# Writing the folded tiles of an FFT-like mixing stage component-major instead of feature-major

## The chip, the cores and the metric

The kernel runs on one core of a Trainium2 chip. The time is device microseconds (us) of one execution of the whole program, and the figure given for a kernel is the median of its runs. Engines are called by the profile's short names: PE (TensorE matmul) with PEld (its weight load), DVE (VectorE), ACT (ScalarE), POOL (GpSimd) and SP (SyncE).

## The reference, cut to what matters

Two dense transforms of an input `x` of 8 x 3072 x 256, of which the real part goes into a feed-forward layer with a maximum over three projections:

```python
X = np.fft.fft(x, axis=1)          # x: (8, 3072, 256), over the 3072 positions
X = np.fft.fft(X, axis=2)          # over the 256 features
a = X.real.reshape(24576, 256)
h = np.maximum(np.maximum(a @ w1, a @ w2), a @ w3)   # w1, w2, w3: (256, 768)
out = h @ w_out                                      # w_out: (768, 256)
```

## The kernel before, in words

The work goes batch by batch, 8 batches of 3072 positions. A batch has a transform part (`fnet`) and a feed-forward part of three blocks of 512 columns (the loop over `blk`), each with 6 chunks `jc` of the 768 hidden features.

`fnet` splits the length-3072 transform as 24 x 128. Its steps, with the lines that the prediction uses:

- Stage 1 (L270): 64 matmuls per batch transform 24 points, with columns of `x0` as the stationary operand. Each result group goes through a PSUM tile of the pool `ps_f`, which has two buffers, and ACT casts it to bf16 into `ub` (L272), in 13 pieces per batch in the order of the table `DLS`.
- The fold (L280, and single columns at L289 to L297): DVE adds and subtracts mirrored feature columns of `ub` and writes the sums into `zE` and the differences into `zO`. In `ub` 24 components of one feature lie side by side. Per batch there are 4 instructions of 25 x 24 elements, 8 of 10 x 24 and 8 of 9 x 24, half of each into `zE`. They can start as the pieces of `ub` arrive: first features 20 to 44, then 10 to 19 and 45 to 54, then the rest.
- Stage 2 (L318, L321 on `zE`; L324, L326 on `zO`; L332 to L334 for the middle position): 128-point transforms. Each matmul takes one component r of all 128 folded features as its stationary operand, `er[:, :, r]` or `orr[:, :, r]`. They fill six PSUM tiles per batch from the same two buffers of `ps_f` (three for `zE`, three for `zO`, 8 or 10 matmuls each), and ACT casts each to bf16 `tE` or `tO` (L329). So the third tile can be filled only when ACT has cast the first, and so on.

One matmul of stage 2 needs every feature of `zE` (or `zO`), so the first L318 waits for the last instruction of the fold that writes `zE`, the copy at L292.

The feed-forward part of a block: L349 and L350 (and L357 for the mirrored half) into PSUM tiles `pse`, ACT's Relu into `stmp` (L363), DVE's maximum into `hp` or `hm` (L364), and then the output products L367, L369 and 6 times L372 into the PSUM tile `po` of a pool with two buffers, which DVE copies to `ot` (L392) and SP stores.

What sets the order: on each engine instructions run in the order in which the building framework's scheduler put them, which is fixed when the kernel is built. The output products of the earlier block stand in a queue (`l2_queue`), so the scheduler has matmuls at hand to put between those of `fnet`; they are called fillers below. A new `po` can be written only when DVE has copied the one before the last.

Of the kernel before, what the change touches and what calls it, by code (L numbers as in the profile page):

```python
# [34 lines left out]
def kernel(  # L35
# [16 lines left out]
    nc = tc.nc  # L52
# [44 lines left out]
    def load_x0(b, between):  # L97
        x0 = x0_pool.tile([96, 128 * 64], BF16, name="x0", tag="x0")
        xr = x[b].rearrange("(a bb) (g dl) -> g a bb dl", bb=128, g=4)
        x0v = x0.rearrange("p (bb dl) -> p bb dl", dl=64)  # L100
        for ch in range(4):
            if ch in between:
                between[ch]()
            for g in range(4):
                nc.gpsimd.dma_start(  # L105
                    out=x0v[g * 24:(g + 1) * 24, ch * 32:(ch + 1) * 32, :],
                    in_=xr[g, :, ch * 32:(ch + 1) * 32, :])
        return x0
# [15 lines left out]
    dvec = gen.tile([128, 128], FP32, tag="dvec")  # L124

    def between():

        nc.gpsimd.iota(kidx, [[1, 13], [24, 128]], base=0, channel_multiplier=0,
                       allow_small_or_imprecise_dtypes=True)
        nc.gpsimd.iota(dvec, [[1, 64], [64, 2]], base=0, channel_multiplier=0,  # L130
                       allow_small_or_imprecise_dtypes=True)

    with tc.manual_schedule(engines={mybir.EngineType.Pool}):
# [80 lines left out]
    zO_tiles = [consts.tile([128, 128 * 26], BF16, name=f"zO{i}", tag=f"zO{i}")  # L214
                for i in range(1)]
    for zO in zO_tiles:
        nc.vector.memset(zO.rearrange("p (c r) -> p c r", r=26)[:, :, 24:26], 0.0)
        nc.vector.memset(zO[:, 0:26], 0.0)

    def prep_first():  # L220

# [42 lines left out]
    def fnet(b, x0):  # L264
# [9 lines left out]
        u = ub.rearrange("p (dl g r) -> p dl g r", g=4, r=24)  # L274
        zE = z_pool.tile([128, 128 * 24], BF16, name="zE", tag="zE")
        zO = zO_tiles[b % len(zO_tiles)]
        e = zE.rearrange("p (dl g r) -> p dl g r", g=2, r=24)
        o = zO.rearrange("p (dl g r) -> p dl g r", g=2, r=26)
        def fold(dst, op, lo, hi, g):
            nc.vector.tensor_tensor(out=dst[:, lo:hi, g, 0:24], in0=u[:, lo:hi, g, :],  # L280
                                    in1=u[:, 64 - lo:64 - hi:-1, 3 - g, :], op=op)
# [14 lines left out]
        nc.vector.tensor_copy(o[:, 0, 0, 13:24], u[:, 0, 2, 1:12])  # L296
        nc.vector.tensor_copy(o[:, 0, 0, 24:26], u[:, 0, 2, 0:13:12])  # L297

        er = zE.rearrange("p (c r) -> p c r", r=24)
        orr = zO.rearrange("p (c r) -> p c r", r=26)  # L300

        def iO(r):
            return 24 if r == 0 else 25 if r == 12 else 12 + r
# [121 lines left out]

    for b in range(B):
        tt = fnet(b, x0_tiles.pop(b))
        if b == 0:
            prep_first()
# [60 lines left out]
```

## Time and profile before

| | |
|---|---|
| median of 3 runs | 500.29 us (499.56 to 500.31) |
| the profiled execution's own time | 499.23 us |
| its span, first to last instruction | 497.1 us |
| mean granted TensorE clock | 0.993 |
| busy: PE, PEld, DVE, ACT, POOL | 453.5, 315.6, 320.4, 260.9, 140.6 us |

Matmuls are pipelined: their records overlap, so how fast PE goes is read from the distance between starts and not from the length of a record. In a timeline the first number of a row is the start and the second how long the row's instructions took together, both in us; a bracket says how long the engine sat idle before and what released it.

### The profile page before, as it was taken

What the parts mean: (1) busy time and instruction counts of PE and PEld (TensorE: products, weight loads), DVE (VectorE), ACT (ScalarE), POOL (GpSimd) and SP (SyncE); (2) the same over time, 40 slices, a digit from 0 to 9 for tenths busy, and PEclk for the clock granted to TensorE, in tenths of its full rate; (3) what the DMA queues carried; (4) which work ended last, traced back from release to release, by engine and by line L of the source; (5) the groups of instructions that cost most, each with busy time, mean ns of one, the idle gap of its engine ahead of it and who ended that gap; (6) DMA issues with size and microseconds to landing.
All of it is one profiled execution on the core that took longest, in us unless ns stands there. A gap on an engine that the chain in (4) does not pass through costs nothing.

```text
span 497.1 us, 9195 instructions
## 1 busy us (share of the span) xinstructions
PE 453.5 (91%) x3408; PEld 315.6 (63%) x3408; DVE 320.4 (64%) x662; ACT 260.9 (52%) x472; POOL 140.6 (28%) x160
## 2 busy tenths in 40 slices
PE   0056999999999999999999999999999999999995
PEld 0055447785568657785669666875669566866664
DVE  8834674657676576657666567657675666667663
ACT  1355652575436653575446644665457644765440
POOL 9979800029000750029000840048000100020000
PEclk9999899999999999999999999999999999999998
DMA  8999992219921692219911793119911022102122
GB/s 48 75 164 99 98 32 86 84 44 108 105 86 66 59 133 99 73 44 109 126 65 65 74 123 102 65 46 120 134 64 65 22 65 84 65 22 65 65 84 86
DMA packets 163436, 40.05 MB, mean 81 GB/s; under 512 B 136512, under 2 KB 163392, under 8 KB 163392
## 3 DMA queue, kind: packets, MB, share of 16 engines
q0 software_dynamic: 135536, 14.30, 70.6%
q1 hardware_dynamic: 27856, 25.18, 16.1%
q8 instruction: 26, 0.43, 0.4%
q14 instruction: 18, 0.15, 0.1%
HBM read 28.31 MB, written 25.17 MB: 108 GB/s over the span
## 4 chain that ended last, share of the span: by engine, by line
PE 78%; DVE 3%; ACT 2%; POOL 2%; DMA 1%; issue 1%; DVEq 0%; ACTq 0%
PE po L372 23%; PE pse L349 12%; PE pse L357 11%; PE pse L350 11%; PE ps L270 8%; PE po L367 4%; PE po L369 4%; POOL x L105 2%; PE ps L318 2%; DMA x<-in_x_dram 1%; PE ps L324 1%; PE ps L326 1%; ACT stmp L363 1%; PE ps L321 1%; DVE zE L280 1%
## 5 line engine op out<-in xcount | busy, mean ns | idle before, releaser
L363 ACT ACTIVATE stmp<-pse 128x512 bf16<-128x512 f32 (+1 forms) x294 | 167.7, 588 | 164.3 <-PE pse L350 128.6
L364 DVE TENSOR_TENSOR hp<-pse,stmp 128x512 bf16<-128x512 f32 x144 | 99.1, 690 | 99.1 <-PE pse L357 39.8
L105 POOL DMA_DIRECT2D x<-in_x_dram x128 | 109.5, 863 | 8.1 <-DMA x<-in_x_dram 3.6
L349 PE MATMUL pse<-tE,gE 128*128 128x512 bf16 x288 | 108.8, 379 | 1.7 <-DVE hm L364 0.7
L350 PE MATMUL pse<-tO,gO 128*128 128x512 bf16 x288 | 109.1, 380 | 0.0
L364 DVE TENSOR_TENSOR hm<-pse,stmp 128x512 bf16<-128x512 f32 x144 | 99.0, 687 | 11.8 <-ACT stmp L363 9.3
L357 PE MATMUL pse<-tO,gD 128*128 128x512 bf16 x288 | 94.8, 380 | 1.1 <-ACT stmp L363 0.6
L339 POOL COPY tEr<-tE 128x1536 bf16<-128x1536 bf16 x8 | 11.8, 1471 | 289.1 <-ACT tE L329 289.1
L372 PE MATMUL po<-wout_bf,hp 128*128 128x256 bf16 x576 | 92.6, 272 | 0.0
L372 PE MATMUL po<-wout_bf,hm 128*128 128x256 bf16 x576 | 89.1, 272 | 0.1
L270 PE MATMUL ps<-m24blk,x 96*128 96x96 bf16 x512 | 57.4, 250 | 28.8 <-DMA w_bf<-in_moe_w_dram 27.5
L270 PEld LDWEIGHTS <-x 96*128 96x128 bf16 x512 | 55.9, 199 | 33.1 <-DMA w_bf<-in_moe_w_dram 27.4
L392 DVE COPY ot<-po 128x512 f32<-128x512 f32 x96 | 65.5, 684 | 14.5 <-PE po L372 13.8
L372 PEld LDWEIGHTS <-hm 128*128 128x128 bf16 x576 | 56.1, 99 | 17.3 <-DVE hm L364 0.4
L372 PEld LDWEIGHTS <-hp 128*128 128x128 bf16 x576 | 56.2, 100 | 14.2
L272 ACT CAST ub<-ps 128x480 bf16<-128x480 f32 (+1 forms) x104 | 55.4, 554 | 15.6 <-PE ps L270 13.3
L357 PEld LDWEIGHTS <-gD 128*128 128x128 bf16 x288 | 28.1, 98 | 29.8 <-issue 1.5
L350 PEld LDWEIGHTS <-gO 128*128 128x128 bf16 x300 | 29.4, 98 | 27.1 <-issue 12.2
L349 PEld LDWEIGHTS <-gE 128*128 128x128 bf16 x300 | 29.5, 99 | 21.1 <-issue 2.6
L280 DVE TENSOR_TENSOR zE<-ub 128x240 bf16<-128x240 bf16 (+2 forms) x80 | 20.2, 311 | 33.9 <-ACT ub L272 33.9
L367 PE MATMUL po<-gw,tE 128*128 128x256 bf16 x96 | 26.2, 272 | 0.0
L369 PE MATMUL po<-gwr,tOr 128*128 128x256 bf16 x96 | 26.2, 272 | 0.0
(99 smaller groups left out, 359.5 us busy)
## 6 DMA issues: line engine op xcount, KB each, us to landing
out_dram<-ot SPq DMA_DIRECT2D x176, 128.0 KB, 1.7
x<-in_x_dram POOLq DMA_DIRECT2D x128, 96.0 KB, 6.7
out_dram<-ot SPq DMA_DIRECT2D x24, 64.0 KB, 6.7
w_bf<-in_moe_w_dram POOLq DMA_DIRECT2D x6, 192.0 KB, 6.2
out_dram<-ot SPq DMA_DIRECT2D x8, 63.0 KB
wout_bf<-in_moe_w_out_dram POOLq DMA_DIRECT2D x1, 384.0 KB, 8.6
out_dram<-ot SPq DMA_DIRECT2D x1, 8.0 KB
```

The source lines that it names most:

```text
L105: nc.gpsimd.dma_start(out=x0v[g * 24:(g + 1) * 24, ch * 32:(ch + 1) * 32, :], in_=xr[g, :, ch * 32:(ch + 1) * 32, :])
L270: nc.tensor.matmul(ps1[:, i * 96:(i + 1) * 96], x0r[:, :, d0 + i], m24blk, start=True, stop=True)
L272: nc.scalar.copy(out=ub[:, d0 * 96:d1 * 96], in_=ps1[:, 0:(d1 - d0) * 96])
L349: nc.tensor.matmul(pse[:, 0:n], gE[i][:, js], te, start=True, stop=False)
L350: nc.tensor.matmul(pse[:, 0:n], gO[i][:, js], to, start=False, stop=True)
L357: nc.tensor.matmul(pse, gD[i][:, js], to, start=False, stop=True, skip_group_check=True)
L363: nc.scalar.activation(out=stmp[:, 0:n], in_=pses[0][:, 0:n], func=AX.Relu)
L364: nc.vector.tensor_tensor(out=dst, in0=src3, in1=stmp[:, 0:n], op=ALU.max)
L367: nc.tensor.matmul(po, te, gw[:, 0:256], start=True, stop=False)
L369: nc.tensor.matmul(po, to, wo, start=False, stop=False)
L372: nc.tensor.matmul(po, hcols(jc), wout_bf[:, jc * 256:(jc + 1) * 256], start=False, stop=(jc == NJC - 1))
L392: nc.vector.tensor_copy(out=ot, in_=po)
```

## The change

`zE` and `zO` keep their sizes, but the order of their elements changes. Before, element (feature c = 2 dl + g, component r) stood at c x 24 + r (26 for `zO`); now the component is the outer index and the feature c = 64 g + dl the inner one. The table `dvec` that builds the second transform's matrix follows the new numbering of features, and the two zeroing memsets follow the new places.

```diff
-        nc.gpsimd.iota(dvec, [[1, 64], [64, 2]], base=0, channel_multiplier=0,
+        nc.gpsimd.iota(dvec, [[1, 128]], base=0, channel_multiplier=0,
...
-        nc.vector.memset(zO.rearrange("p (c r) -> p c r", r=26)[:, :, 24:26], 0.0)
-        nc.vector.memset(zO[:, 0:26], 0.0)
+        nc.vector.memset(zO[:, 24 * 128:26 * 128], 0.0)
+        nc.vector.memset(zO.rearrange("p (r c) -> p r c", c=128)[:, :, 0:1], 0.0)
...
-        e = zE.rearrange("p (dl g r) -> p dl g r", g=2, r=24)
-        o = zO.rearrange("p (dl g r) -> p dl g r", g=2, r=26)
+        e = zE.rearrange("p (r g dl) -> p dl g r", g=2, r=24)
+        o = zO.rearrange("p (r g dl) -> p dl g r", g=2, r=26)
...
-        er = zE.rearrange("p (c r) -> p c r", r=24)
-        orr = zO.rearrange("p (c r) -> p c r", r=26)
+        er = zE.rearrange("p (r c) -> p c r", r=24)
+        orr = zO.rearrange("p (r c) -> p c r", r=26)
```

Two access patterns follow. A stationary operand `er[:, :, r]` was 128 elements 48 bytes apart (52 for `zO`) and is now 128 neighbours. The fold's output, walked component by component inside a feature, was runs of 24 neighbours and is now single elements 256 bytes apart; its two inputs stay runs of 24 neighbours.

The scheduler puts some instructions elsewhere. On DVE, in the second batch, the fold stood so before (names are tiles, `x2` is two alike in a row):

```order
L280 TENSOR_TENSOR zE<-ub 128x25x24 x2
L280 TENSOR_TENSOR zO_248<-ub 128x25x24 x2
L392 COPY ot<-po 128x512
L280 TENSOR_TENSOR zE<-ub 128x10x24 x4
L280 TENSOR_TENSOR zO_248<-ub 128x10x24 x4
L280 TENSOR_TENSOR zE<-ub 128x9x24 x4
```

and now, from the same place to the first maximum behind the fold:

```order
L280 TENSOR_TENSOR zO_248<-ub 128x25x24 x2
L280 TENSOR_TENSOR zE<-ub 128x10x24 x4
L280 TENSOR_TENSOR zO_248<-ub 128x10x24 x4
L280 TENSOR_TENSOR zE<-ub 128x9x24 x4
L289 TENSOR_TENSOR zE<-ub 128x24
L292 COPY zE<-ub 128x24
L280 TENSOR_TENSOR zO_248<-ub 128x9x24 x4
L289 TENSOR_TENSOR zO_248<-ub 128x24
L294 TENSOR_SCALAR zO_248<-ub 128x11
L296 COPY zO_248<-ub 128x11
L297 COPY zO_248<-ub 128x2
L392 COPY ot<-po 128x512 x2
```

The copy of a finished `po` that stood inside the fold now stands behind it, next to the other one.

On PE, just ahead of stage 2 of the second batch (minus is before, plus is now):

```order
-L367 LDWEIGHTS tE
-L367 MATMUL po<-gw,tE 128x256
-L369 LDWEIGHTS tO
-L369 MATMUL po<-gw,tO 128x256
-L372 LDWEIGHTS hp
-L372 MATMUL po<-wout_bf,hp 128x256
-L372 LDWEIGHTS hp
-L372 MATMUL po<-wout_bf,hp 128x256
-L372 LDWEIGHTS hp
-L372 MATMUL po<-wout_bf,hp 128x256
 L318 LDWEIGHTS zE
 L318 MATMUL ps_1078<-cos_t,zE 128x128
```

Five fillers no longer stand ahead of the first L318; they come behind stage 2 (five in the second batch, four in the third, six in each later one). And inside stage 2, still on PE, between the second and the third tile of `zE`:

```order
 L321 LDWEIGHTS zE
 L321 MATMUL ps_1088<-sin_t,zE 128x128
-L372 LDWEIGHTS hp
-L372 MATMUL po<-wout_bf,hp 128x256
-L372 LDWEIGHTS hp
-L372 MATMUL po<-wout_bf,hp 128x256
 L318 LDWEIGHTS zE
 L318 MATMUL ps_1098<-cos_t,zE 128x128
```

The two fillers that stood there in every batch from the second on have gone behind stage 2 too. The first batch has no fillers, before or now.

## The prediction

> **What bounds the kernel now.** I read the page's busy times and the chain that ended last, then the waits, then the timeline of DVE, ACT and PE around one batch's stage 2 (the third batch; the later ones repeat it within 0.1 us).
>
> ```profile
> PE 453.5 (91%) x3408; PEld 315.6 (63%) x3408; DVE 320.4 (64%) x662; ACT 260.9 (52%) x472; POOL 140.6 (28%) x160
> ...
> PE 78%; DVE 3%; ACT 2%; POOL 2%; DMA 1%; issue 1%; DVEq 0%; ACTq 0%
> ...
> PEld L318 <- DVE zE L292: 4.7, 8, 1.8
> ```
>
> PE carries 78% of the chain. The third row counts that in all 8 batches stage 2 waits for the fold's last write to `zE`. The 4.7 us look harmless, but the wait says that the fold ends last there: whatever lengthens it, PE sits out, unless fillers stand ahead.
>
> The third batch, DVE first, then ACT:
>
> ```profile
> 155.24 0.85 DVE L280 TENSOR_TENSOR zE<-ub 128x600 bf16<-128x600 bf16 x2 [2.37 <-ACT ub L272]
> 156.01 0.84 DVE L280 TENSOR_TENSOR zO<-ub 128x600 bf16<-128x600 bf16 x2
> 156.77 0.68 DVE L392 COPY ot<-po 128x512 f32<-128x512 f32 x1
> 157.76 0.87 DVE L280 TENSOR_TENSOR zE<-ub 128x240 bf16<-128x240 bf16 x4 [0.31 <-ACT ub L272]
> 158.55 0.86 DVE L280 TENSOR_TENSOR zO<-ub 128x240 bf16<-128x240 bf16 x4
> 160.24 0.81 DVE L280 TENSOR_TENSOR zE<-ub 128x216 bf16<-128x216 bf16 x4 [0.84 <-ACT ub L272]
> 160.97 0.16 DVE L289 TENSOR_TENSOR zE<-ub 128x24 bf16<-128x24 bf16 x1
> 161.05 0.16 DVE L292 COPY zE<-ub 128x24 bf16<-128x24 bf16 x1
> ...
> 162.08 0.16 DVE L297 COPY zO<-ub 128x2 bf16<-128x2 bf16 x1
> ...
> 159.65 0.56 ACT L272 CAST ub<-ps 128x480 bf16<-128x480 f32 x1 [0.29 <-PE ps L270]
> 162.14 1.09 ACT L329 CAST tE<-ps 128x512 bf16<-128x512 f32 x2 [1.93 <-PE ps L321]
> 163.50 0.59 ACT L329 CAST tE<-ps 128x512 bf16<-128x512 f32 x1 [0.27 <-PE ps L318]
> 164.11 0.59 ACT L329 CAST tO<-ps 128x512 bf16<-128x512 f32 x1
> ```
>
> The fold has slack inside: it waits 0.31 and 0.84 us for `ub` and carries one copy of `po`. Its `zE` is ready at 161.05 + 0.16 = 161.21, its `zO` at 162.24. PE at the same place:
>
> ```profile
> 160.32 0.27 PE L369 MATMUL po<-gw,tO 128*128 128x256 bf16 x1
> 160.43 0.71 PE L372 MATMUL po<-wout_bf,hp 128*128 128x256 bf16 x5
> 161.27 0.28 PE L318 MATMUL ps<-cos_t,zE 128*128 128x128 bf16 x1
> 161.39 0.24 PE L321 MATMUL ps<-sin_t,zE 128*128 128x128 bf16 x1
> 161.47 0.23 PE L318 MATMUL ps<-cos_t,zE 128*128 128x128 bf16 x1
> 161.53 0.23 PE L321 MATMUL ps<-sin_t,zE 128*128 128x128 bf16 x1
> ...
> 165.68 0.20 PE L334 MATMUL ps<-cos_t,zO 128*128 128x1 bf16 x1
> 165.75 0.38 PE L349 MATMUL pse<-tE,gE 128*128 128x512 bf16 x1
> ```
>
> Fillers start 0.11 apart, so the last of them is through at 160.43 + 5 x 0.11 = 160.98 and PE idles 0.29 before 161.27. Stage 2 then lasts to 165.75, 4.48 us with 0.65 us of other matmuls in it.
>
> **The change part by part: the stationary loads.** Loads, strided and not, and the starts of two small matmuls with neighbouring columns:
>
> ```profile
> L372 PEld LDWEIGHTS <-hp 128*128 128x128 bf16 x576 | 56.2, 100 | 14.2
> L318 PEld LDWEIGHTS <-zE 128*128 128x128 bf16 x104 | 14.6, 162 | 4.8 <-DVE zE L292 4.7
> L270 PEld LDWEIGHTS <-x 96*128 96x128 bf16 x512 | 55.9, 199 | 33.1 <-DMA w_bf<-in_moe_w_dram 27.4 <-issue 3.1 <-DMA x<-in_x_dram 0.5
> 480.77 0.17 PE L349 MATMUL pse<-t_mid,gE 128*128 128x8 bf16 x1
> 480.80 0.17 PE L350 MATMUL pse<-t_mid,gO 128*128 128x8 bf16 x1
> ```
>
> Stage 2's matmuls start 0.07 apart. The stream does not explain that: 256 columns take 0.11 (rows of L369 and L372 above), so 128 take 0.0555. The strided load (162 ns against 100) sets it, and with neighbouring columns starts can be 0.03 apart. So after the change 44 matmuls of 128 columns save 0.0145 (`zE`) or 0.011 (`zO`) each, and the nine narrow ones some 0.035: 22 x 0.0145 + 22 x 0.011 + 9 x 0.035 = 0.88 us of PE per batch.
>
> Most of it does not reach the end, because ACT empties the two PSUM buffers. After the change, counted from stage 2's start S: the eighth matmul starts at 0.44, ACT begins its cast at 0.77 (before: 161.27 to 162.14, 0.87) and ends at 1.36, one cast takes 0.545 in a row or 0.59 alone (rows at 162.14 and 163.50). The second tile is done by 0.95, so the third waits from 0.95 to 1.41 and ends at 1.80; an L349 to 2.02; the first of `zO` to 2.47; the second waits for ACT to 2.74 and ends at 3.19; an L349; the third 3.40 to 3.85; the middle position waits to 4.10 and ends at 4.19. The 0.88 turn into 0.46 + 0.27 + 0.25 of waiting. Stage 2 lasts 4.19 where it lasted 4.48, and holds 0.43 of other matmuls where it held 0.65. Net of those it is 0.07 us shorter, per batch.
>
> **The fold.** How fast does DVE go now, and with scattered single writes?
>
> ```profile
> L182 DVE TENSOR_TENSOR v<-v,q 128x1664 f32<-128x1664 f32 x2 | 3.7, 1882 | 0.0
> L364 DVE TENSOR_TENSOR hp<-pse,stmp 128x512 bf16<-128x512 f32 x144 | 99.1, 690 | 99.1 <-PE pse L357 39.8 <-ACT stmp L363 32.2 <-PE pse L350 26.7
> L217 DVE MEMSET zO<- 128x128 uint32 x1 | 0.2, 165 | 0.1
> ```
>
> Two 600s start 0.77 / 2 = 0.385 apart and four 240s 0.79 / 4 = 0.1975, so 0.52 ns per element and 0.0725 fixed. Operations on f32 take (1882 - 690) / (1664 - 512) = 1.035 ns per element, twice as much. So the fold handles two bf16 elements in the time of one, and its output must be neighbours for two to be written together; 256 bytes apart they aren't. No row shows this output. Lower bound: nothing changes, 0.52. Upper bound: one element at a time, and each write to a far place slowed as the farthest strided load is, 199 / 100, so 2.1 ns. I take 1.04, one at a time without a penalty, by the nearest row: the memset wrote 128 words 52 bytes apart in 165 ns, at most 1.29 ns each. [...]
>
> Starts then lie 0.0725 + 0.625 = 0.698 apart for 600s, 0.322 for 240s, 0.2975 for 216s. From 155.24: four 600s to 158.03 (`ub` is there since 157.76), eight 240s to 160.61 (the last `ub` lands at 159.65 + 0.56 = 160.21), four 216s to 161.80, L289 0.09, L292 0.16: `zE` at 162.05, 0.84 later. The lost packing costs 4 x 0.313 + 8 x 0.125 + 4 x 0.113 = 2.7 us up to there; the copy that moved away and the two waits for `ub` give 1.9 back. `zO` follows at 163.5, which is S + 1.4 and ahead of its use at S + 2.02. The two copies of `po` behind it end near 164.8, ahead of the next maximum.
>
> **The fillers.** The five to six that moved behind stage 2 (mean 0.61 us) and the two inside it (0.22) are not lost work, but at their old places PE now stands still. S = 162.11; PE has run dry at 160.98 - 0.66 = 160.32 and idles 1.79 instead of 0.29. Stage 2 ends at 162.11 + 4.19 = 166.30 instead of 165.75: 0.55 later, with 0.83 us of matmuls (mean of the batches) still to do. Where these then stand decides: into gaps of the first block, or between matmuls that have none.
>
> ```profile
> 166.00:205.00 39.00, 38.76 (x244) 23.65 (x243) 27.57 (x42) 19.27 (x36) 14.29 (x17) 1.00 1.00 96
> ```
>
> PE's records leave only 0.24 of 39 us free behind stage 2 (second column, PE's busy time); records overlap, so wider starts hide in them, and I take half of the 0.83 as absorbed. Ends: none, 1.38 per batch; all, 0.55; the middle 0.97.
>
> **The first batch** has no fillers and no matmul gain:
>
> ```profile
> 31.23 0.85 DVE L280 TENSOR_TENSOR zE<-ub 128x600 bf16<-128x600 bf16 x2 [8.72 <-ACT ub L272]
> 37.08 0.16 DVE L292 COPY zE<-ub 128x24 bf16<-128x24 bf16 x1
> 37.43 0.31 PE L321 MATMUL ps<-sin_t,zE 128*128 128x128 bf16 x1
> 37.54 0.31 PE L318 MATMUL ps<-cos_t,zE 128*128 128x128 bf16 x1
> ```
>
> Starts are 0.11 apart there, twice the 0.0555 of 128 columns, and the records last 0.31 instead of 0.23: the stream is slow there and sets the pace, not the load. The same sum from 31.23 gives `zE` at 38.04 instead of 37.24: 0.8 us. The memsets and the table cost nothing: they run while PE waits 27 us for its first data (the row of L270 above).
>
> **Sum:** 0.8 + 7 x 0.97 = 7.6 us on the profiled execution's 499.23 (span 497.1 and 2.1 around it): 506.8. The median shown is 1.06 above that execution, which would give 507.9; I say 507.5. Its own range: 0.8 + 7 x 0.55 = 4.7 to 0.8 + 7 x 1.38 = 10.5, so 503.9 to 510.8.
>
> **The rivals.** *The fold keeps its pace* (other side). If scattered output doesn't break the pairing, `zE` comes at 161.21 as before, stage 2 ends 0.29 earlier, and with every moved filler absorbed the kernel is 7 x 0.29 = 2 us faster: 497.2 to 498.3; with none absorbed 3.8 slower. Faster needs `zE` to come under 0.29 us later. For it: no row shows the output in question. Against: the 0.52 against 1.04 ns. 8 in 100 (faster 5, same 2, slower 1).
>
> *Scattered writes cost more than one at a time.* At 2.1 ns starts are 1.34, 0.58 and 0.53 apart, `zE` comes 6.4 us later, and 8 batches give some 50 us: 550. For it: strided loads on PE take up to twice as long. Against: the memset. [...] 6 in 100.
>
> *The clock drops.* The granted clock (third column from the end of the second row) fell to half once, after a gap:
>
> ```profile
> 48.46 0.81 PE L232 MATMUL psg<-v_bf,md 128*128 128x384 bf16 x4 [3.05 <-DVE v_bf L228]
> 49.90:53.10 3.20, 3.20 (x10) 1.31 (x9) 2.21 (x5) 1.08 (x3) 3.20 (x5) 0.50 1.65 98
> ```
>
> PE would idle 1.8 us per batch and three times 0.3 to 0.5 soon after. If that brings half clock for the 3.4 us seen there, it costs 1.7 x 7 = 12 us more: 519. Against: 1.8 is well under 3.05. 6 in 100.
>
> **The numbers.** Main case 80 in 100, rivals 8, 6 and 6. 502.5 to 513 leaves out the rivals, 2 in 10, and gives the main case's ends some room. About 0.2% (1 us) is what a measurement can tell from no change: faster 0.05; same 0.04 (2 of the rival, 2 of a main case with all absorbed and an earlier `zE`); slower 0.91.
>
> **What the profile after would show.** Right: L280 at 600 elements 780 ns (now 468), at 240 about 400; loads of `zE` and `zO` near 100 ns, stage 2's starts 0.056 apart; the wait PEld L318 for `zE` 13 to 17 us instead of 4.7; ACT's L329 still 0.55 to 0.6 each and PE waiting for them inside stage 2. Wrong if L280 stays under 500 ns or passes 1000, if the wait stays under 6, or if the granted clock falls inside later batches.

## The result: 657.7 us, almost a third slower, and the profile after

| | before | after |
|---|---|---|
| median (range), runs side by side | 499.93 us (498.83 to 500.31) | 657.70 us (656.90 to 657.94) |
| ratio, 95% interval | | 1.3158 (1.3133 to 1.3183) |
| span of the profiled execution | 497.1 us | 655.7 us |
| mean granted TensorE clock | 0.993 | 0.891 |

The forecast was 507.5 us, 502.5 to 513: the sign was right, the size wrong by a factor of 20. The page of the kernel after (busy times, clock in 40 slices, chain by engine):

```profile
PE 460.3 (70%) x3408; PEld 319.6 (49%) x3408; DVE 504.3 (77%) x662; ACT 261.4 (40%) x472; POOL 136.5 (21%) x160
...
PEclk9999999679995899869996699959998699968999
...
PE 53%; DVE 30%; POOL 2%; ACT 2%; issue 2%; DMA 1%; DVEq 0%; ACTq 0%
```

DVE is 184 us busier (504.3 against 320.4) and its share of the chain went from 3% to 30%, while PE does the same work. The clock, near full before, dips once per batch. The groups of the kernel after, by shape (busy, mean ns of one, then the idle time before them and what ended it):

```profile
L280 DVE TENSOR_TENSOR zE<-ub 128x600 bf16<-128x600 bf16 x16 | 44.0, 2940 | 19.8 <-ACT ub L272 19.8
L280 DVE TENSOR_TENSOR zE<-ub 128x240 bf16<-128x240 bf16 x32 | 37.1, 1445 | 0.0
...
L318 PEld LDWEIGHTS <-zE 128*128 128x128 bf16 x104 | 14.7, 146 | 147.8 <-DVE zE L292 147.8
L324 PEld LDWEIGHTS <-zO 128*128 128x128 bf16 x104 | 12.1, 117 | 19.5 <-DVE zO L294 17.1 <-DVE zO L296 2.5
L270 PEld LDWEIGHTS <-x 96*128 96x128 bf16 x512 | 55.0, 200 | 26.8 <-DMA w_bf<-in_moe_w_dram 22.9 <-issue 2.1
```

A fold instruction of 600 elements takes 2940 ns where it took 468, and stage 2 waits 147.8 us for `zE` where it waited 4.7. The waits alone account for the loss: `zE` 147.8 - 4.7 = +143.1, `zO` 19.5 from 0, the first data 22.9 - 27.4 = -4.5; together +158.1, and the span grew by 158.6. All the rest, the faster loads, the lower clock and what was moved among it, adds up to half a microsecond. The timeline of the second batch, DVE and then PE:

```profile
111.11 5.50 DVE L280 TENSOR_TENSOR zE<-ub 128x600 bf16<-128x600 bf16 x2 [1.62 <-ACT ub L272]
116.23 5.71 DVE L280 TENSOR_TENSOR zO<-ub 128x600 bf16<-128x600 bf16 x2
121.57 4.64 DVE L280 TENSOR_TENSOR zE<-ub 128x240 bf16<-128x240 bf16 x4
...
134.04 0.43 DVE L292 COPY zE<-ub 128x24 bf16<-128x24 bf16 x1
...
134.53 0.29 PE L318 MATMUL ps<-cos_t,zE 128*128 128x128 bf16 x1 [18.05 <-DVE zE L292]
134.61 0.31 PE L321 MATMUL ps<-sin_t,zE 128*128 128x128 bf16 x1
134.71 0.31 PE L318 MATMUL ps<-cos_t,zE 128*128 128x128 bf16 x1
...
139.51 0.23 PE L324 MATMUL ps<-nsin_t,zO 128*128 128x128 bf16 x1 [1.93 <-DVE zO L296]
```

No wait for `ub` interrupts the fold any more and no copy of `po` stands in it: from 111.11 to 134.47 DVE does nothing else. The four 600s take 121.57 - 111.11 = 10.46, their starts lie 2.67 us apart in the middle of a run: 4.44 ns per element, where it was 0.52 and a fixed part. PE, out of fillers, idles 18 us. Then it runs slowly: starts 0.107 apart in the `zE` part. The windows of the kernel after show why (third column from the end: granted clock):

```profile
118.00:120.00 2.00, 0.00 (x0) 0.00 (x0) 2.00 (x2) 0.00 (x0) 0.00 (x0) 1.00 0.00 0
120.00:122.00 2.00, 0.00 (x0) 0.00 (x0) 2.00 (x2) 0.00 (x0) 0.00 (x0) 0.61 0.00 0
134.50:136.00 1.50, 1.48 (x15) 1.48 (x16) 1.50 (x2) 0.40 (x1) 0.00 (x0) 0.50 0.00 0
137.50:140.91 3.41, 1.47 (x20) 1.11 (x20) 3.26 (x7) 1.01 (x3) 1.47 (x1) 1.00 0.00 0
```

PE has stopped at 134.53 - 18.05 = 116.48. Some 4 us later (1.9 to 4.8 in the batches behind it) the clock falls to half (0.61 on average in the second row: full for 0.22 of the row's 2 us, to 120.44) and is still there when stage 2 begins. Once it is back (last row), stage 2's starts on `zO` lie 0.056 apart, as forecast.

### The profile page after: what moved, and what is told of

Read it like the earlier page. It is cut to its first block, busy times and chain, and to the rows that moved or that the text cites. A ratio compares the mean times of both kernels' runs of the same rounds, so it can differ in the third digit from the quotient of the medians.

```text
span 655.7 us, 9227 instructions
## 1 busy us (share of the span) xinstructions
PE 460.3 (70%) x3408; PEld 319.6 (49%) x3408; DVE 504.3 (77%) x662; ACT 261.4 (40%) x472; POOL 136.5 (21%) x160
## 4 chain that ended last, share of the span: by engine, by line
PE 53%; DVE 30%; POOL 2%; ACT 2%; issue 2%; DMA 1%; DVEq 0%; ACTq 0%
PE po L372 17%; DVE zO L280 14%; DVE zE L280 13%; PE pse L349 9%; PE pse L357 9%; PE pse L350 9%; PE po L367 3%; PE po L369 3%; PE ps L270 2%; POOL x L105 2%; PE ps L324 1%; DMA x<-in_x_dram 1%; DVE zO L294 1%; PE ps L326 1%; ACT stmp L363 1%
## 5 line engine op out<-in xcount | busy, mean ns | idle before, releaser
L280 DVE TENSOR_TENSOR zE<-ub 128x240 bf16<-128x240 bf16 (+2 forms) x80 | 114.9, 1701 | 19.8 <-ACT ub L272 19.8
L318 PE MATMUL ps<-cos_t,zE 128*128 128x128 bf16 (+1 forms) x104 | 21.3, 298 | 145.7 <-DVE zE L292 145.7
L280 DVE TENSOR_TENSOR zO<-ub 128x240 bf16<-128x240 bf16 (+2 forms) x80 | 116.6, 1723 | 0.0
L349 PE MATMUL pse<-tE,gE 128*128 128x512 bf16 x288 | 111.9, 390 | 1.6 <-ACT stmp L363 0.4
L105 POOL DMA_DIRECT2D x<-in_x_dram x128 | 106.0, 836 | 7.8 <-DMA x<-in_x_dram 4.5
L357 PE MATMUL pse<-tO,gD 128*128 128x512 bf16 x288 | 92.4, 379 | 0.7 <-ACT stmp L363 0.3
L318 PEld LDWEIGHTS <-zE 128*128 128x128 bf16 x104 | 14.7, 146 | 147.8 <-DVE zE L292 147.8
L329 ACT CAST tE<-ps 128x512 bf16<-128x512 f32 x24 | 14.0, 585 | 159.6 <-PE ps L321 158.1
L392 DVE COPY ot<-po 128x512 f32<-128x512 f32 x96 | 65.1, 683 | 11.0 <-PE po L372 10.7
L270 PE MATMUL ps<-m24blk,x 96*128 96x96 bf16 x512 | 56.0, 250 | 24.2 <-DMA w_bf<-in_moe_w_dram 22.9
L270 PEld LDWEIGHTS <-x 96*128 96x128 bf16 x512 | 55.0, 200 | 26.8 <-DMA w_bf<-in_moe_w_dram 22.9
```

What stands on the lines that cost most here:

```text
L105: nc.gpsimd.dma_start(out=x0v[g * 24:(g + 1) * 24, ch * 32:(ch + 1) * 32, :], in_=xr[g, :, ch * 32:(ch + 1) * 32, :])
L270: nc.tensor.matmul(ps1[:, i * 96:(i + 1) * 96], x0r[:, :, d0 + i], m24blk, start=True, stop=True)
L318: nc.tensor.matmul(outsl, er[:, :, r], cos_t[:, k0:k0 + w], start=True, stop=not two)
L349: nc.tensor.matmul(pse[:, 0:n], gE[i][:, js], te, start=True, stop=False)
L357: nc.tensor.matmul(pse, gD[i][:, js], to, start=False, stop=True, skip_group_check=True)
L392: nc.vector.tensor_copy(out=ot, in_=po)
```

## The experiments

Two theories were open. *The writes:* a lone 2-byte element written far from its neighbour is what costs, and everything else follows from PE's wait. *The arrangement:* something else in the change (the loads, the moved fillers, the 256-byte step, a power of two) does it.

| kernel | median us (range) | ratio to before (95%) | 600s start apart, ns | load of `zE`, ns | wait for `zE`, us |
|---|---|---|---|---|---|
| before | 499.67 and 500.25 | | 387 | 162 | 4.7 |
| loads only | 493.17 (491.52 to 495.06) | 0.9872 (0.9840 to 0.9904) | 387 | 104 | 3.5 |
| fold only | 662.42 (661.64 to 663.06) | 1.3266 (1.3226 to 1.3306) | 2667 | 166 | 147.0 |
| loops exchanged | 539.20 (538.03 to 541.01) | 1.0802 (1.0765 to 1.0839) | 1163 | 147 | 44.9 |
| pairs | 494.88 (494.67 to 495.17) | 0.9890 (0.9871 to 0.9909) | 617 | 104 | 4.8 |
| fours | 496.75 (495.60 to 497.67) | 0.9926 (0.9908 to 0.9945) | 389 | 117 | 4.7 |
| eights | 497.44 (495.64 to 498.64) | 0.9936 (0.9913 to 0.9959) | 386 | 148 | 4.6 |

The first three share one chip's runs of the kernel before (499.67), the last three another's (500.25). The load column is a mean over the run. Where the clock fell in stage 2 it holds slowed loads: in the kernel after, a load of 128 neighbours takes 98 ns at full clock (139.5 to 140.3) and 151 at half (134.6 to 136.8), and the 147 with exchanged loops (mean clock 0.956) and the 166 of the fold alone (0.884) hold such loads too.

**Loads alone.** The fold and its layout as before; only the loads read neighbours, so they read the wrong elements and the values differ.

```diff
-        er = zE.rearrange("p (c r) -> p c r", r=24)
-        orr = zO.rearrange("p (c r) -> p c r", r=26)
+        er = zE.rearrange("p (r c) -> p c r", r=24)
+        orr = zO.rearrange("p (r c) -> p c r", r=26)
```

> The kernel before with its own packed fold; only stage 2's stationary operands are taken as 128 neighbouring elements, so they hold other elements than the transform needs and the output is not the reference's. Theory of the prediction's stage-2 step (ACT's casts take back nearly all of PE's gain): loads of zE near 100 ns instead of 162, starts 0.056 apart, and the whole 0 to 2 us shorter than before. Rival (PE's gain comes through): 0.88 us for each of 7 batches, 5 to 6 us shorter.

It is faster by 6.5 us, more than either outcome that I named. Part of this is not due to faster loads: in the layout of before, the 128 neighbours that the first L318 loads hold only a few features, and it starts when these are written. In every batch it starts 0.47 us before the fold's last copy into `zE` ends, where in the kernel before it starts 0.06 after it. So what the loads give is read inside stage 2. Timeline of the third batch, first and last matmul of stage 2 and ACT's casts:

```profile
159.92 0.23 PE L318 MATMUL ps<-cos_t,zE 128*128 128x128 bf16 x1
...
163.83 0.16 PE L334 MATMUL ps<-cos_t,zO 128*128 128x1 bf16 x1
...
161.86 0.59 ACT L329 CAST tE<-ps 128x512 bf16<-128x512 f32 x1 [0.15 <-PE ps L318]
162.46 1.87 ACT L329 CAST tO<-ps 128x512 bf16<-128x512 f32 x3
```

From the first L318 to the last L334 it takes 3.91 us, where before it took 4.41 (161.27 to 165.68). Both hold the same 0.65 us of other matmuls (of one L349 only the load is recorded, at 162.15), so stage 2 is 0.50 shorter. ACT still sets its end: the second cast of `tO` is done at 162.46 + 2 x 0.623 = 163.71, and the middle position follows at 163.78. So 0.50 of PE's 0.88 come through in a batch, where I let 0.07 through. Over all batches, the way from the first L318 of the first batch to that of the eighth shrank from 398.88 to 394.81 us, 0.58 per batch, the early start included. (This profiled execution, 494.37, is 1.2 above the median.)

**The fold alone.** The new fold and layout; the loads keep the old strides over the same bytes, so the values differ here too.

```diff
-        e = zE.rearrange("p (dl g r) -> p dl g r", g=2, r=24)
-        o = zO.rearrange("p (dl g r) -> p dl g r", g=2, r=26)
+        e = zE.rearrange("p (r g dl) -> p dl g r", g=2, r=24)
+        o = zO.rearrange("p (r g dl) -> p dl g r", g=2, r=26)
```

> The other half alone: the fold writes component-major as in the changed kernel, stage 2 keeps the strided loads of before (so it reads other elements than it needs). If the fold's writes alone make the loss: within 4 us of the changed kernel's 657.7. If the loads, or loads and writes together, had a part in it: at least 10 us away from it.

```profile
L280 DVE TENSOR_TENSOR zE<-ub 128x600 bf16<-128x600 bf16 x16 | 44.0, 2940 | 20.8 <-ACT ub L272 20.8
...
L318 PEld LDWEIGHTS <-zE 128*128 128x128 bf16 x104 | 16.7, 166 | 147.0 <-DVE zE L280 147.0
```

The groups of this kernel show the whole wait with slow loads. The difference to the changed kernel, 662.42 - 657.70 = 4.7 us, is a little more than the 4 that I allowed and far from 10: without the fast loads the loss is as large, and they are worth about 5 us beside it.

**What a write costs.** Behind the end of the kernel before, with all engines idle, three operations each of 240 bf16 elements, contiguous inputs, and outputs at different steps; the output of the kernel is unchanged. This battery and the next are one execution each. Of the form

```diff
+    for _ in range(3): nc.vector.tensor_tensor(out=to(scr, 128), in0=ia, in1=ib, op=ADD)
```

where the second number is the step in elements.

> The kernel before, and behind a barrier at its end three each of 240-element bf16 additions with the output's inner step at 2, 32, 52, 64, 128, 192, 240, 256, 258, 260, 264, 272, 288, 320, 384 and 512 bytes, further pairs of neighbours 256 bytes apart, copies, a memset, f32 outputs, strided inputs, and ACT's copies. The changed kernel's fold took 4.44 ns per element at 256 bytes. Theory A (a step that is a power of two, or a multiple of 64 bytes, sends all writes to one place of the memory): 52, 258, 260, 264 and 272 bytes near 1.04 ns, 64, 128, 256 and 512 near 4.4. Theory B (each write of 2 bytes to another 16-byte line costs the same): 4.4 ns at every step of 32 bytes or more. Theory C (a write of less than 4 bytes is slow by itself when alone): the f32 outputs and the pairs near 1.04 to 2.2 ns per written word at 256 bytes, bf16 4.4 at every step. Reads 128 or 256 bytes apart: 1.04 ns if only writes suffer.

The timeline, of DVE except for the last row. L483 writes neighbours; L484, L485, L490 and L494 lone elements 32, 52, 256 and 272 bytes apart; L499 writes 240 pairs 256 bytes apart; L501 is a copy and L502 a memset, both of lone elements (272 and 256 bytes apart), L503 an addition that writes neighbours; L505 reads both inputs at 256 bytes and writes neighbours; L510 is ACT's copy with the writes of L490.

```profile
496.91 0.92 DVE L483 TENSOR_TENSOR scr<-tE,tO 128x240 bf16<-128x240 bf16 x3 [4.23 <-SPq L465]
497.86 3.55 DVE L484 TENSOR_TENSOR scr<-tE,tO 128x240 bf16<-128x240 bf16 x3
501.45 3.74 DVE L485 TENSOR_TENSOR scr<-tE,tO 128x240 bf16<-128x240 bf16 x3
...
520.55 3.75 DVE L490 TENSOR_TENSOR scr<-tE,tO 128x240 bf16<-128x240 bf16 x3
...
535.46 3.73 DVE L494 TENSOR_TENSOR scr<-tE,tO 128x240 bf16<-128x240 bf16 x3
...
554.08 1.76 DVE L499 TENSOR_TENSOR scr<-tE,tO 128x480 bf16<-128x480 bf16 x3
...
558.28 2.16 DVE L501 COPY scr<-tE 128x240 bf16<-128x240 bf16 x3
561.37 0.26 DVE L502 MEMSET scr<- 128x240 bf16 x1 [0.93 <-DVE scr L501]
...
563.75 0.26 DVE L502 MEMSET scr<- 128x240 bf16 x1 [0.93 <-DVE scr L502]
564.05 0.92 DVE L503 TENSOR_TENSOR scr<-tE,tO 128x240 bf16<-128x240 bf16 x3
...
566.94 2.14 DVE L505 TENSOR_TENSOR scr<-zE,zO 128x240 bf16<-128x240 bf16 x3
...
575.20 3.83 ACT L510 COPY sca<-scr 128x240 bf16<-128x240 bf16 x3
```

Contiguous, one operation follows the other after 0.317 us; with lone elements after 1.20 at 32 bytes and 1.26 at 256; over all 15 steps tried, from 32 to 512 bytes, it was 1.19 to 1.39. The theory of the power of two falls: 272 bytes cost what 256 do. On ACT it is no better (3.83 for three, 1.24 contiguous). A DVE copy, with one input, took 0.73 to 0.86 with lone elements; why less stays open. Pairs, 240 whole 4-byte words, take 0.60, and so do 240 f32 outputs 256 bytes apart. Taking 0.317 - 240 x 0.52 ns = 0.19 as fixed, a lone element costs (1.26 - 0.19) / 240 = 4.4 ns and a lone word (0.60 - 0.19) / 240 = 1.7 ns. Reading both inputs at 256 bytes costs half as much, (0.72 - 0.19) / 240 = 2.2. And a record of a memset, such as my nearest row, is no price: each of the three lasts 0.26, but DVE sits idle for 0.93 ahead of each, ahead of the first (behind the copy) too, while L503 follows 0.04 after the last. From start to start it is 1.19; the part that the record leaves out lies ahead of it.

**What makes it dear.** The same arrangement with other outputs.

> The kernel before, and behind its end, when all engines are idle, DVE adds two bf16 operands of 192 to 240 contiguous elements and writes the result in 15 forms, three times each; the output is unchanged. What makes a lone element dear? Known from the battery before: a lone 2-byte element costs 4.4 to 5 ns at any step from 32 bytes on, a lone 4-byte word 1.7 to 2 ns, a contiguous element 0.52 plus some 0.15 us for the operation. Theory W, it is the part of a 4-byte word: single elements cost 4 to 5 ns (240 in about 1.2 us) at steps of 4, 8, 16 bytes too; at even and at odd places alike; pairs that fill a word take about 1.7 ns a word (120 words in 0.25 to 0.36 us), but pairs that lie across two words make two partial words each, 8.8 ns a pair (over 1 us); triples hold one partial word however they lie, 72 x (4.4 + 0.5) = about 0.4 to 0.5 us both ways; quads 0.2 to 0.25 us aligned and 0.45 us or more when shifted by 2 bytes. Theory L, it is the visit to another line of 32 bytes, whatever is written there: single elements get cheaper below a step of 32 bytes (16 bytes 2.2 ns, 8 bytes 1.1 ns, 4 bytes 0.55 ns), and aligned and shifted pairs, triples and quads cost the same. Theory R, it is a run of one: single elements 4.4 ns at every step above 2 bytes, any run of two or more is cheap wherever it lies.

DVE's timeline: L484, L485, L486 write lone elements 4, 8 and 16 bytes apart (L484 ran alternately with L489, lone elements 256 bytes apart, and their records overlap). Then groups, each 256 bytes from the one before: L490 pairs in one word, L491 pairs across two words, L492 triples, L494 fours from a word's start, L495 fours shifted by 2 bytes, L497 eights shifted by 2 bytes.

```profile
496.15 1.22 DVE L489 TENSOR_TENSOR scr<-tE,tO 128x240 bf16<-128x240 bf16 x1
496.99 0.66 DVE L484 TENSOR_TENSOR scr<-tE,tO 128x240 bf16<-128x240 bf16 x1
497.54 1.21 DVE L489 TENSOR_TENSOR scr<-tE,tO 128x240 bf16<-128x240 bf16 x1
...
499.72 2.39 DVE L485 TENSOR_TENSOR scr<-tE,tO 128x240 bf16<-128x240 bf16 x3
502.14 3.73 DVE L486 TENSOR_TENSOR scr<-tE,tO 128x240 bf16<-128x240 bf16 x3
...
513.29 1.16 DVE L490 TENSOR_TENSOR scr<-tE,tO 128x240 bf16<-128x240 bf16 x3
514.48 2.15 DVE L491 TENSOR_TENSOR scr<-tE,tO 128x240 bf16<-128x240 bf16 x3
516.66 1.50 DVE L492 TENSOR_TENSOR scr<-tE,tO 128x216 bf16<-128x216 bf16 x3
...
519.74 0.84 DVE L494 TENSOR_TENSOR scr<-tE,tO 128x192 bf16<-128x192 bf16 x3
520.62 1.51 DVE L495 TENSOR_TENSOR scr<-tE,tO 128x192 bf16<-128x192 bf16 x3
...
523.04 1.19 DVE L497 TENSOR_TENSOR scr<-tE,tO 128x192 bf16<-128x192 bf16 x3
```

Less the fixed 0.19, an aligned pair costs 1.7 ns, a shifted one 4.5; a triple 4.5; an aligned four 2.1 (nothing above contiguous), a shifted one 6.7; a shifted eight 9.1. The same data at the same distances costs up to three times as much when it leaves a 4-byte word half written. So the part of a word decides whether the high price is paid, as theory W says, and the run of one (R) falls.

How often it is paid does not follow W, which named 8.8 for a shifted pair and 4.4 for lone elements at every step. L484 ends 0.27 us after the L489 ahead of it (497.65 against 497.37), so at 4 bytes an element costs 1.1 ns, and the 0.66 of its record is no price. At 8 bytes the second and third L485 take 0.73 to the next start, 2.2 ns; at 16 bytes it is 1.25, 4.4 ns. That is theory L's proportion with a line of 16 bytes instead of 32. The two together fit all these additions: about 4.4 ns for each piece of 16 bytes in which a word is left half written, however many elements lie in it. At steps of 4, 8 and 16 bytes four, two and one lone elements share a piece. A shifted pair or a triple lies within one (counted from the start of `scr`), every second shifted four lies across two, 1.5 x 4.4 = 6.6, and so does each shifted eight, 2 x 4.4 = 8.8. This is a fit to these rows: the copies, at about 2.4 ns per lone element, do not follow it, and how the chip writes half a word these runs don't show.

**The loops exchanged.** The layout after, but the fold walks features innermost: the writes are runs, and now the two inputs are read 192 bytes apart.

```diff
-            nc.vector.tensor_tensor(out=dst[:, lo:hi, g, 0:24], in0=u[:, lo:hi, g, :],
-                                    in1=u[:, 64 - lo:64 - hi:-1, 3 - g, :], op=op)
+            nc.vector.tensor_tensor(
+                out=dst[:, lo:hi, g, 0:24].rearrange("p dl r -> p r dl"),
+                in0=u[:, lo:hi, g, :].rearrange("p dl r -> p r dl"),
+                in1=u[:, 64 - lo:64 - hi:-1, 3 - g, :].rearrange("p dl r -> p r dl"), op=op)
```

> The changed kernel with the fold's loops exchanged: the same elements, but each instruction walks the features inside a component, so the output is runs of 9 to 25 neighbours and the inputs step 192 bytes. If only scattered writes are slow and reads go one element per 1.04 ns: the L280 near 780 ns at 600 elements and 504 to 511 us, what the prediction forecast for one element at a time. If scattered reads cost as the writes do: 640 us or more.

```profile
L280 DVE TENSOR_TENSOR zE<-ub 128x600 bf16<-128x600 bf16 x16 | 19.5, 1258 | 19.8 <-ACT ub L272 19.8
...
L320 PEld LDWEIGHTS <-zE 128*128 128x128 bf16 x104 | 14.8, 147 | 44.9 <-DVE zE L294 44.9
```

The groups show that the fold needs 1163 / 600 = 1.94 ns per element and PE waits 44.9 us, 40.2 more than before; the kernel is 39.5 slower. That lies between the two outcomes that I named: reads cost neither 1.04 nor as much as the writes, and 1.94 is near the battery's strided reads. Better than scattered writes, and still bound by the fold. This run also settles the second theory: its layout and its loads are those of the kernel after, DVE's instructions and PE's weight loads stand in the same order, and only the way in which one fold instruction walks its elements differs. With that, 657.70 - 539.20 = 118.5 us of the loss are gone, so neither the moved fillers nor the 256-byte step of the layout makes them.

**Pairs, fours, eights.** The layout between the two: Q components of one feature stay neighbours, then come the other features. The fold writes runs of Q, a load reads elements 2Q bytes apart. In the code, for Q = 2:

```diff
-        e = zE.rearrange("p (dl g r) -> p dl g r", g=2, r=24)
+        Q = 2
+        e = zE.rearrange("p (k dl g j) -> p dl g k j", g=2, k=12, j=Q)
...
-                        nc.tensor.matmul(outsl, er[:, :, r], cos_t[:, k0:k0 + w],
+                        nc.tensor.matmul(outsl, zcol(ev, r), cos_t[:, k0:k0 + w],
```

> The kernel before with components kept in pairs: element (feature c, component r) of zE and zO stands at (r // 2) x 256 + 2 c + r % 2. The fold then writes whole 4-byte words 512 bytes apart, stage 2 loads elements 4 bytes apart. Theory C (only a write of less than a 4-byte word is slow, 4.4 ns; a lone word takes 1.68 ns as in the battery): 0.84 ns per element, L280 near 660 ns at 600 elements, zE 0.7 us later per batch, loads gain about as much back: 495 to 502 us. Rival (each lone visit to another 16-byte line costs 4.4 ns, whatever its width): 2.2 ns per element, L280 near 1450 ns, and 540 us or more as with exchanged loops.

> The same with components in fours, runs of 8 bytes in the fold and elements 8 bytes apart in the loads. Theory C with a write per run of 1.68 ns at most: 0.42 ns per element, under the 0.52 of the packed fold, so L280 stays near 470 ns at 600 elements. If loads 8 bytes apart run like neighbours (near 100 ns): 491 to 495 us, as with the loads alone. If they cost as those 48 bytes apart (162 ns): 498 to 501.

> The same with components in eights, runs of 16 bytes in the fold and elements 16 bytes apart in the loads. Fold as before, L280 near 470 ns. If a load pays for each visit to another 16-byte line, its loads take 150 ns or more and the time is 498 to 501 us; if only steps beyond 16 bytes cost, 491 to 495.

All three are faster than both kernels, pairs most: 494.88 us. Pairs come out 0.1 us below the range that I named, fours between my two cases and eights 0.6 below theirs. DVE's timeline of the third batch with pairs:

```profile
153.09 1.34 DVE L284 TENSOR_TENSOR zE<-ub 128x600 bf16<-128x600 bf16 x2 [2.36 <-ACT ub L272]
...
155.44 0.65 DVE L415 COPY ot<-po 128x512 f32<-128x512 f32 x1
156.03 1.05 DVE L284 TENSOR_TENSOR zE<-ub 128x240 bf16<-128x240 bf16 x4
...
158.93 0.17 DVE L302 COPY zE<-ub 128x24 bf16<-128x24 bf16 x1
```

The fold runs at 617 / 600 = 1.03 ns per element, where it was 387 / 600 = 0.65, and still `zE` is ready 158.93 + 0.17 - 153.09 = 6.01 us after its start, against 5.97 before: the slower writes fill the time in which the fold waited for `ub`. Loads take 104 ns and stage 2 lasts 3.91 us as with the loads alone, here without the early start: its first matmul comes 0.06 after the last copy into `zE`. From the second batch to the eighth the distance between stages 2 shrinks by 0.47 us per batch (331.14 to 328.32 over six). With eights the loads take 148 ns and starts 0.060, with fours 117 ns and 0.056: a load at a step of 8 bytes does not show in the starts yet. That pairs beat fours by 1.9 us is no matter of the fold: behind the first batch both have the same distances between stages 2 (55.8 and 55.8, 54.99 and 54.93, down to 53.98 and 53.99). The difference lies before the second batch, where the windows of the kernel before and of pairs show

```profile
50.00:56.00 6.00, 5.79 (x23) 2.58 (x22) 4.21 (x9) 3.25 (x8) 6.00 (x9) 0.73 2.07 106
```

```profile
50.00:56.00 6.00, 5.32 (x29) 2.72 (x28) 3.98 (x8) 4.69 (x11) 6.00 (x8) 1.00 3.99 88
```

With pairs PE's gap ahead of L232 is 2.13 us, and the clock stays full; before it was 3.05 and with fours 3.50, and the clock fell (0.73 and 0.78 in this window). In these executions the first two stages 2 lie 65.64 us apart with pairs and 68.61 with fours. But the clock does not explain 494.88: the mean granted clock of the five executions with pairs goes from 0.994 to 0.997, and their times agree within 0.5 us, without order. Whether pairs save time there by design or by the luck of the first transfers stays open.

## Why the prediction was wrong, by its own steps

- **The fold's price: the step that failed.** I took 1.04 ns per element, between 0.52 and 2.1. It is 4.44. That the pace of before needs neighbours was borne out: at a step of 4 bytes a lone element costs 1.1 ns, in pairs it is 1.03, in fours 389 / 600 = 0.65 as before. What the forecast said of the path came true: `zE` comes later, PE has run out of fillers, and it sits out the delay. The term was too small. The upper end came from PE's strided loads, another engine that reads, and the nearest row for the choice was the memset of 128 words 52 bytes apart, 165 ns. That row misled twice: a memset's record can leave out most of its time (0.26 of 1.19 us for 240 elements), so 1.29 ns was no upper limit, and it wrote whole words, which cost an addition 1.7 ns, where the fold writes halves of words at 4.4. With 4.44 the prediction's own sum, four 600s, eight 240s and four 216s, gives 10.7 + 8.5 + 3.8 us and the small ones 0.3: 23.3, as measured (111.11 to 134.47), and with 5.97 before 17 us later per batch.
- **The rival "scattered writes cost more"** had the mechanism and the sign, with 6 in 100. Its price stopped at 2.1 and so its time at 550. The strided loads (162 and 199 ns against 100), which I weighed against the memset, spoke for it. In the runs lone elements cost an addition 1.1, 2.2 and 4.4 ns at steps of 4, 8 and 16 bytes, and 4.2 to 5.0 from 32 to 512. Whole words at far places cost 1.7.
- **`zE` 0.84 us later at 1.04 ns** was wrong as well, in the other direction. Pairs run at 1.03 ns per element and `zE` comes 0.04 later. I had carried the fixed 0.0725 of the fast form over to the slow one (0.698 per 600; measured 0.617, and 0.24 against 0.322 per 240). Without it the prediction's own sum puts `zE` about 0.15 later (an estimate from the rows of the prediction). At about the price I forecast, pairs are 5 us faster, not 7.6 slower; but they keep fillers ahead of stage 2 and the copy of `po` inside the fold, as the kernel before does, so what the changed kernel would do at that price stays open. That the sign came out right is no merit of the sum: it rests on a price four times the one in it.
- **ACT takes nearly all of PE's gain** failed in size. With the loads alone, the loads (104 ns) and the starts (0.056), from which the 0.88 us of PE follow, were right, and ACT does set stage 2's end. But my sum let ACT begin its third cast at S + 2.15 (2.74 less one cast of 0.59); it began at 1.94, and the two fillers stand in the wait that was left, so stage 2 lasted 3.94 to the next L349 with 0.65 of other matmuls in it, not 4.19 with 0.43. That ACT starts sooner behind the narrow matmuls (0.2 after the last one's start, 0.3 behind a full tile) is the likely reason.
- **The fillers'** cost of 0.97 per batch can't be seen. No run moved them alone, and in the slow kernels the loads' gain and the lower clock hide them. Open.
- **The clock** was a rival for itself (6 in 100) at an idle of 1.8 us. It fell, because the idle was 18. Half clock doubles the distance of some 24 starts in the `zE` part, 24 x 0.051 = 1.2 us per batch. (The starts 0.11 apart and the records of 0.31 that the prediction found in the first batch are those of half clock here.) At 1.9 us it goes both ways: after the gap ahead of `zO` the clock fell in the second batch (139.51, half clock from 140.9 on) and not in the eighth. The traces' own record of the granted clock shows more: in those of the two kernels the clock changes only at times that lie a whole multiple of 3.41 us apart, in the kernel before at 49.80, 53.22 and 493.54, in the kernel after at 120.43, 137.50, 140.91, 144.32, 195.52 and so on. The fall goes with how much of one such stretch PE is idle. The rows show the stretch behind that of 137.50 to 140.91 (above), then two in the eighth batch:

```profile
140.92:144.32 3.40, 3.40 (x20) 1.75 (x19) 0.69 (x1) 2.08 (x5) 1.87 (x2) 0.50 0.46 154
594.90:598.29 3.39, 1.82 (x29) 1.54 (x30) 2.76 (x7) 1.07 (x2) 1.40 (x1) 1.00 0.10 34
598.31:601.70 3.39, 3.39 (x23) 1.67 (x20) 1.98 (x3) 2.27 (x6) 1.47 (x1) 1.00 0.36 119
```

The second batch's gap lies whole in the stretch from 137.50 to 140.91, in which PE's records leave 3.41 - 1.47 = 1.94 us free, and half clock follows. The eighth's (594.51 to 596.41) began in the stretch before; 3.39 - 1.82 = 1.57 are left, and the clock stays. In these two traces every recorded stretch at full clock with 1.87 us free or more was followed by half clock, and none with 1.59 or less; none lies between.
- **What would show it:** where the clock was full, the loads (98 ns) and the starts came as named; L280 passed 1000 ns and the granted clock fell in later batches, two of the signs for "wrong".

## What to carry to other kernels

Look at the smallest piece that an access pattern writes: on this chip a bf16 element alone costs an addition on DVE 4.2 to 5.0 ns, whatever the step from 16 to 512 bytes (ACT's copies at 52 to 272 bytes take as long, 1.29 us for 240), and two that fill a 4-byte word cost 1.7 (2.06 in the fold). So when a layout must be turned between a writer and a loader, keep pairs together: the load at a 4-byte step was as fast as a contiguous one (104 ns), and the fold lost only time that it had spent waiting. And when no row of a profile shows an operation, take the range from the same engine and the same direction, and price it by the distance between the starts of several alike, not by the record.

## What was not expected of the hardware

- A lone bf16 write costs 4.4 ns, eight times a contiguous one (0.52), where "one at a time" would be 1.04; at steps of 4 and 8 bytes it is 1.1 and 2.2 ns.
- A memset of lone bf16 elements has a record of 0.26 us, and 0.93 us in which DVE seems idle stand ahead of it.
- A bf16 load at 4 bytes takes 104 ns, at 8 bytes 117, at 16 bytes 148, at 48 bytes 162; the starts show it only from 16 bytes on (0.060, and 0.070 at 48).
- In the traces of the two kernels the granted clock changed only at times a whole multiple of 3.41 us apart. In the seven idle stretches of 18 us for which it is on record it stayed full for 1.9 to 4.8 us, and in the second batch it came back after 3.0 us of work at half clock (134.5 to 137.5). A gap of 1.9 us was enough for half clock when it lay whole between two such times.
